# Column blocks of 256 and 225 instead of 251 and 250 in a fused Fourier mixing and MLP kernel

## The chip, the cores and the metric

One core of a Trainium2 chip runs the whole kernel in one launch. The metric is the device time of one execution in microseconds, as the median of several runs. The kernel before takes 1913.87 us.

## The reference

The input `x` is 8 x 3008 x 256, float32. The output is a two-layer MLP with a squared ReLU, applied to the real part of a two-dimensional Fourier transform of each of the eight batches:

```python
X = np.fft.fft(x, axis=1)
X = np.fft.fft(X, axis=2)
h = X.real.reshape(8 * 3008, 256) @ w_in      # w_in: 256 x 2048
g = np.maximum(h, 0.0) ** 2
out = g @ w_out                               # w_out: 2048 x 256
```

## The kernel before

**Two halves.** For each batch b a transform along the sequence makes three tables: `Pt`, `Qt` and `Et`, with 128, 127 and 128 partitions and `NKT` = 1505 columns each, one column for each frequency from 0 to 1504. The transform along the 256 features is multiplied into `w_in` once, at the start (L344, a float32 product with 256 columns of a tile `win`), which gives the weights `G1` and `G2`. The hidden values at frequency k and at its mirror, 3008 - k, are then a sum and a difference of the same two products, so that 1505 columns give 3008 tokens.

**The main loop** runs over the batches (8), over the column blocks of `CK` columns (`BLOCKS`, six a batch: five of 251 and one of 250) and over j (8 pairs of 128 hidden units). One pass through it is a step; there are 384. A step consists of:

- `front`: for each of the two hidden chunks h a product of `Pt` (L881, 128 rows) and one of `Qt` (L882, 127 rows) with `n` columns into one PSUM tile `ph` (two buffers). VectorE then makes the sum and the difference of the two in three instructions (L892, L894, L895), written to a tile `g` with four parts: g11, g12, g21, g22. L895 is the last to read `ph`.
- `relu` and `square` on ScalarE (L906, L909), each over all four parts of `g`.
- `combine` on GpSimd (L916 to L919): four sums of parts of `g` into a tile `s`. They serve a scheme in the manner of Strassen, which makes the second layer with seven products in place of eight.
- `back`, two steps later: seven products (L947) with `n` columns of `g` or `s` into four PSUM tiles `mA` to `mD`, which accumulate over j. (The very first block uses eight plain products, L932.)

So a step has 11 float32 matmuls. The tiles of moving operands are allocated with `CK` columns to a part:

```python
g = gp.tile([P, 2, 2, CK], F32, name="g", tag="g")
s = sp.tile([P, 4, CK], F32, name="s", tag="s")
ks = slice(k0, k0 + n)    # the columns of Pt and Qt in this block
```

With `CK` = 251 part k of `g` or `s` starts at float 251 k of its tile, and block m of `Pt` and `Qt` at float 251 m.

After the eighth j `gather` evicts the four PSUM tiles, and `store` transposes the block on VectorE in squares of 32 (L1018 for the full squares, L1019 for the rest) and sends it out over the SyncE queue, for each of the two mirrored sides. The last block of the kernel is transposed on TensorE instead (L1002).

**The order** is written out by hand. A list of tokens (`ORDER`) sets it for the first ten steps, amid the conversion of the weights. Later, `between` puts pieces of the next batch's fold and transform (L510 to L808) between the steps. Each piece has a written cost, and `pace` and `SHARE` spread them by the number of steps, not by their time; `room` lets in up to 1.9 of these units, meant as microseconds, at once. Neither depends on `CK`.

Of the kernel before, what the change touches and what calls it, by code (L numbers as in the profile page):

```python
# [9 lines left out]
F32 = mybir.dt.float32  # L10
# [4 lines left out]
P = 128  # L15
R = 32
# [46 lines left out]
def column_counts(S):  # L63

    counts = []
    for kp in range(2):
        n0 = len(range(kp, S // 4 + 1, 2))
        n1 = (n0 + 1) // 2
        n2 = (n1 + 1) // 2
        counts.append((n2, n2, n1, n0))  # L70
    return counts
# [12 lines left out]
def kernel(  # L84
# [12 lines left out]
    nc = tc.nc  # L97
# [3 lines left out]
    NKT = M + 1  # L101
# [2 lines left out]
    H = D // 2  # L104
    NJ = NFC // 2
    CH = 256
    CK = 251
    NX = 3
    TILES = class_tiles(S)
    NT = len(TILES)  # L110
    NC = column_counts(S)
# [4 lines left out]
    const = ctx.enter_context(tc.tile_pool(name="const", bufs=1))  # L116
# [3 lines left out]
    pq = ctx.enter_context(tc.tile_pool(name="pq", bufs=2))  # L120
    hp = ctx.enter_context(tc.tile_pool(name="hp", bufs=3))
# [3 lines left out]
    op = ctx.enter_context(tc.tile_pool(name="op", bufs=2))  # L125
# [92 lines left out]
    make_identity(nc, ident)  # L218
    last = ident[:, P - 1:]

    signs = const.tile([P, 2], F32, name="signs")
    for i in range(2):
        nc.vector.tensor_scalar(out=signs[:, i:i + 1], in0=last, scalar1=(-2.0, 2.0)[i], scalar2=(1.0, -1.0)[i],
                                op0=ALU.mult, op1=ALU.add)
# [1 line left out]
    lone = wsum.rearrange("p a j h -> p (a j) h")  # L226
    assert 2 * NT <= 3 * NJ
    nc.gpsimd.memset(lone[:, 0:2 * NT], 0.0)
    evens = const.tile([P, 1], F32, name="evens")
    nc.vector.tensor_reduce(out=evens, in_=ident[:, 0::2], op=ALU.add, axis=mybir.AxisListType.X)  # L230
    for c in range(2):
        nc.vector.tensor_scalar(out=sind[:, c, P - 1:], in0=evens, scalar1=2.0, scalar2=-1.0,
# [28 lines left out]
    def scratch():  # L261

        return sp.tile([P, 4 * CK], F32, name="m", tag="s")[:, 0:2 * CH].rearrange("p (c e) -> p c e", c=2)

# [109 lines left out]
    PQE = {}  # L374
# [35 lines left out]
    def columns(tab, t, part):  # L410

        nk, at = NC[0][TILES[t][0]], PLACE[t]
        nq = (nk + 1) // 2
        return tab[:, 0, at + part * nq:at + (nk if part else nq)]

    def quarters(tab, part):

        nk, at = NC[0][3], PLACE[ODD0]
        n4, n2 = (nk + 3) // 4, (nk + 1) // 2
        return tab[0:HALF2, 0, at + part * n4:at + (n2 if part else n4)]  # L420
# [210 lines left out]
    def dft_ops(b):  # L631
# [1 line left out]


        def start():
            PQE[b] = [pq.tile([n, NKT], F32, name=nm, tag=nm)
                      for nm, n in (("Pt", P), ("Qt", P if b == 0 else P - 1), ("Et", P))]

        def group(kp, which):
            both_in = b == 0 and which == 1  # L640
            n = NE if b is None else P - 1 if which == 1 and b else P
            tab = sinT if which == 1 else cosT
            n2, _, n1, n0 = NC[kp]
            st = {}
# [17 lines left out]

            NK1 = (CK + 1) // 2
            EVEN = ((0, 0, n2), (1, n2, n2), (2, 2 * n2, n1))
# [8 lines left out]
                copy_4()  # L673

            def copy_4():
                a = st["a"] = hp.tile([P, 2 * P], F32, name="da", tag="da", bufs=2)[0:n]
                nc.scalar.copy(a[:, 0:n2], st["ps"][0:n, 0:n2])

            def even_part(c, lone_e, only=None):
# [53 lines left out]
            def left(t):  # L733

                if b is None:
                    return we[0:HALF2, SPOT[t], kp]
                return folded[b, t][0:HALF2, kp, PART[which]][:, 0:n]

            def once_more(ps, nk):

                nq = (nk + 2) // 2 if kp else (nk + 1) // 2
                pair = TWO, TWO + 1
                for part in range(2):
                    if kp:
                        tab, o = (cosT, sinT)[part], 0
                        to = ps[:, part * nq:part * nq + nq]
                    else:
                        tab, o = (cosT, sinT)[which], part
                        to = ps[:, part:nk:2]
                    nc.tensor.matmul(to, left(pair[part != which]),  # L750
                                     columns(tab, TWO, o)[0:HALF2], start=True, stop=True)
                if not kp:
                    return ps[:, 0:nk]
                a = hp.tile([P, NC[0][3] // 2 + 1], F32, name="oc", tag="oc", bufs=1)[0:n, 0:nq]
                nc.scalar.copy(a, ps[:, 0:nq])
                return a, ps[:, nq:2 * nq]

            def twice_more(ps):

                av, aw, bv, bw = (left(ODD0 + i) for i in range(4))
                if kp:
                    nq = (n0 + 2) // 2
                    spots = [(tab, part, ps[:, i * nq + part:(i + 1) * nq:2])
                             for i, tab in enumerate((cosT, sinT)) for part in range(2)]
                    ws = (aw, bw, bv, av) if which else (av, bv, bw, aw)
                else:
                    tab = (cosT, sinT)[which]  # L770
                    spots = [(tab, 0, ps[:, 0:n0:4]), (tab, 1, ps[:, 2:n0:4]),
                             (cosT, 0, ps[:, 1:n0 + 1:4]), (sinT, 0, ps[:, 3:n0:4])]
                    ws = (bw, aw, bv, av) if which else (av, bv, aw, bw)
                for (tab, part, to), w in zip(spots, ws):
                    cols = quarters(tab, part)
                    nc.tensor.matmul(to, w, cols[:, cols.shape[-1] - to.shape[-1]:],  # L776
                                     start=True, stop=True)
                ps_a = ps[:, 0:nq] if kp else ps[:, 5:n0 + 1:4]
                a = hp.tile([P, NC[0][3] // 2 + 1], F32, name="oc", tag="oc", bufs=1)[0:n, 0:ps_a.shape[-1]]
                nc.scalar.copy(a, ps_a)  # L780
                if kp:
                    return a, ps[:, nq:2 * nq]
                st["turned"] = a, ps_a, ps[:, 3:n0:4]
                return ps[:, 0:n0]
# [38 lines left out]
            if b == 0:  # L823
                named = [("copy", copy_4), ("join_4", join_4), ("join_2", join_2), ("lo", lambda: join_lo(0, NK1)),
                         ("keep", keep), ("rest", lambda: join_lo(NK1, n0)), ("hi", join_hi)]
                for e in range(2):
                    for t in range(NT):
                        c = TILES[t][0]
# [13 lines left out]
            return ops  # L842

        ops = [] if b is None else [(0.0, start)]
        for which in (0,) if b is None else (0, 1):
            for kp in range(2):
# [5 lines left out]
    def spread_e():  # L852

        _, qt, et = PQE[0]
        ps = psd.tile([P, CH], F32, name="pe", tag="d")[:, 0:CK]
        nc.tensor.matmul(ps, last.to_broadcast([P, P]), qt[:, 0:CK], start=True, stop=True)
        return lambda: nc.scalar.copy(et[:, 0:CK], ps)

    KH = S // 4 + 1

    def spread_lower():
        _, qt, et = PQE[0]
        nc.gpsimd.dma_start(out=e_dram[0:1, CK:KH], in_=qt[P - 1:P, CK:KH])
        nc.gpsimd.dma_start(out=et[:, CK:KH], in_=e_dram[0:1, CK:KH].to_broadcast([P, KH - CK]))
# [124 lines left out]
    def store(b, k0, n, s, c, final):  # L989

        if s == 0:
            row, lo, hi = b * S + k0, 0, n
        else:
            row, lo, hi = b * S + S - (k0 + n - 1), 1 if k0 + n == NKT else 0, n - 1 if k0 == 0 else n
        if final:


            starts = (lo, n - P)
            po = psd.tile([P, 2, H, 2], F32, name="po", tag="d")
            for h in (1, 0) if s else (0, 1):  # L1000
                for i, o in enumerate(starts):
                    nc.tensor.transpose(po[:, i, :, h], c[:, s, h, o:o + P], ident)  # L1002
            os_ = op.tile([P, 2, H, 2], F32, name="os", tag="os")
            for i in range(2):
                (nc.scalar.copy if s or i else nc.vector.tensor_copy)(os_[:, i], po[:, i])
            left = n - lo - P
            last = n - (left if any(left % k == 0 for k in range(9, 17)) else 15 * (P // 16))
            for i, c0, c1 in ((0, lo, lo + P), (1, last, n), (1, lo + P, last)):
                if c0 < c1:
                    (nc.sync if s or i == 0 else nc.scalar).dma_start(out=out[row + c0:row + c1],  # L1010
                                                            in_=os_[c0 - starts[i]:c1 - starts[i], i])
            return


        full, rest = divmod(hi - lo, R)
        os_ = op.tile([P, full + 1, R, 2], F32, name="os", tag="os")
        to = os_.rearrange("p i e h -> p i h e")
        nc.vector.transpose(to[:, 0:full], c[:, s, :, lo:lo + full * R].rearrange("p h (i r) -> p i h r", r=R))  # L1018
        nc.vector.transpose(to[:, full], c[:, s, :, hi - R:hi])  # L1019
        for a in range(P // R):  # L1020
            rows = out[row + lo:row + hi, 2 * R * a:2 * R * (a + 1)]
            part = os_[R * a:R * (a + 1)].rearrange("r i e h -> r i (e h)")
            nc.sync.dma_start(out=rows[0:full * R].rearrange("(i r) d -> r i d", r=R), in_=part[:, 0:full])
            nc.sync.dma_start(out=rows[full * R:], in_=part[R - rest:, full])

    def ahead(b):
        (_, start), *groups = dft_ops(b)
# [288 lines left out]
    for i in range(NJ + LAG, len(steps) + LAG + 4):  # L1316
        if i < len(steps):
            b, k0, n, j = steps[i]
# [19 lines left out]
        if i < len(steps):  # L1338
            relu(n, g)
            square(n, g)  # L1340
            s, ops = combine(n, g)
# [66 lines left out]
```

## Time and profile before

| | |
|---|---|
| median of three runs | 1913.87 us (1913.75 to 1913.92) |
| profiled execution, first to last instruction (span) | 1911.9 us |
| what lies around the span (median less span) | 2.0 us |
| PE busy | 1902.1 us, 9216 passes |
| VectorE / ScalarE / GpSimd busy | 1444.3 / 959.2 / 1132.0 us |
| first pass of the main loop (L881) | 36.7 us after the start |
| HBM traffic | 41.54 MB read, 24.69 MB written |

Of the profiled execution its span is known; the runs' times take in what lies around it. Busy times are sums of instruction lengths, and the lengths of matmul passes overlap: a pass of 251 columns is listed with 374 ns, and the next one starts some 212 ns after it. For TensorE the distance from start to start is therefore what is counted below. The trace holds the start of every pass to the nanosecond; the timeline prints it to 10 ns.

### The profile page before, as it was taken

To read this page: it belongs to the slowest core of one execution; us is meant where nothing else is said; L and a number is where in the kernel's file an instruction comes from. 1 tells how busy PE (TensorE), PEld (TensorE's weight loads), DVE (VectorE), ACT (ScalarE), POOL (GpSimd) and SP (SyncE) were. 2 spreads that over 40 slices of the span, in tenths; PEclk is the share of its full clock that TensorE was granted. 3 is DMA by queue.
4 is the path that set the end of the run, shared out by engine and by line. 5 is a ranking of instruction groups with operands and counts; after the bars stand their busy time and mean duration, and the time that the engine had idled before them with its cause. 6 is when DMAs were issued, how large, how long until landed. Compare 5 with 4: busy or idle time off the path is not lost.

```text
span 1911.9 us, 28094 instructions
## 1 busy us (share of the span) xinstructions
PE 1902.1 (99%) x9216; PEld 1693.9 (89%) x9216; DVE 1444.3 (76%) x3648; ACT 959.2 (50%) x1220; POOL 1132.0 (59%) x1725
## 2 busy tenths in 40 slices
PE   9999999999999999999999999999999999999998
PEld 7888898888988898888988889888898888988887
DVE  8988887787678776888678877788867777655554
ACT  4755555455455454445445554445544545444444
POOL 3265656665566656665665665566655666566565
PEclk9999999999999999999999999999999999999999
DMA  6341211110112101111011100211101101100100
GB/s 193 119 46 25 52 28 36 30 45 12 35 29 47 28 12 36 34 41 28 12 40 43 37 20 14 52 36 28 25 18 43 36 13 21 28 12 11 22 11 22
DMA packets 144381, 68.08 MB, mean 36 GB/s; under 512 B 129176, under 2 KB 134907, under 8 KB 144234
## 3 DMA queue, kind: packets, MB, share of 16 engines
q1 hardware_dynamic: 143646, 65.47, 14.9%
q8 instruction: 72, 1.18, 0.3%
q0 software_dynamic: 448, 0.69, 0.1%
q14 instruction: 76, 0.61, 0.1%
q10 hardware_dynamic: 139, 0.12, 0.0%
HBM read 41.54 MB, written 24.69 MB: 35 GB/s over the span
## 4 chain that ended last, share of the span: by engine, by line
PE 96%; DVE 2%; DMA 1%; ACT 0%; issue 0%; SPq 0%; DVEq 0%; ACTq 0%
PE ph L881 17%; PE ph L882 17%; PE mC L947 17%; PE mA L947 16%; PE mB L947 16%; PE mD L947 8%; PE pd L776 1%; PE mA L932 1%; PE mB L932 1%; PE pd L750 1%; PE pd L658 1%; PE pg L344 0%; DVE w L540 0%; DVE fs L510 0%; DMA raw<-in_moe_w_out_dram 0%
## 5 line engine op out<-in xcount | busy, mean ns | idle before, releaser
L906 ACT ACTIVATE g<-g 128x1004 f32<-128x1004 f32 (+1 forms) x384 | 399.1, 1039 | 691.6 <-DVE g L895 491.8
L892 DVE SCALAR_TENSOR_TENSOR he<-Et,gE,ph 128x251 f32<-128x251 f32 (+1 forms) x768 | 362.4, 472 | 340.9 <-PE ph L882 337.1
L916 POOL TENSOR_TENSOR s<-g 128x251 f32<-128x251 f32 (+1 forms) x376 | 236.7, 630 | 636.9 <-ACT g L909 587.6
L881 PE MATMUL ph<-Pt,G 128*128 128x251 f32 (+1 forms) x1536 | 452.1, 375 | 0.3 <-DVE g L895 0.3
L882 PE MATMUL ph<-Qt,G 127*128 127x251 f32 (+1 forms) x1536 | 451.2, 374 | 0.0
L909 ACT ACTIVATE g<-g 128x1004 f32<-128x1004 f32 (+1 forms) x384 | 399.1, 1040 | 12.0
L947 PE MATMUL mA<-g,wout 128*128 128x251 f32 (+1 forms) x1488 | 376.8, 374 | 0.0
L947 PE MATMUL mC<-s,wsum 128*128 128x251 f32 (+1 forms) x1472 | 373.2, 374 | 0.0
L894 DVE TENSOR_TENSOR g<-he,ph 128x251 f32<-128x251 f32 (+1 forms) x768 | 320.6, 417 | 53.2 <-POOL s L916 1.4
L882 PEld LDWEIGHTS ph<-Qt,G 127*128 127x128 f32 x1536 | 291.3, 190 | 35.7
L881 PEld LDWEIGHTS ph<-Pt,G 128*128 128x128 f32 x1536 | 285.8, 189 | 34.6 <-ACT G L349 0.7
L895 DVE TENSOR_TENSOR g<-he,ph 128x251 f32<-128x251 f32 (+1 forms) x768 | 314.4, 409 | 0.0
L947 PEld LDWEIGHTS mA<-g,wout 128*128 128x128 f32 x1488 | 279.6, 189 | 34.8 <-issue 0.3
L947 PEld LDWEIGHTS mC<-s,wsum 128*128 128x128 f32 x1472 | 279.5, 190 | 33.6
L917 POOL TENSOR_TENSOR s<-s,g 128x251 f32<-128x251 f32 (+1 forms) x376 | 270.7, 720 | 29.5
L918 POOL TENSOR_TENSOR s<-g 128x251 f32<-128x251 f32 (+1 forms) x376 | 272.6, 725 | 0.0
L919 POOL TENSOR_TENSOR s<-g,s 128x251 f32<-128x251 f32 (+1 forms) x376 | 242.3, 644 | 0.0
L947 PE MATMUL mD<-s,wout 128*128 128x251 f32 (+1 forms) x752 | 220.3, 374 | 0.0
L947 PE MATMUL mB<-s,wout 128*128 128x251 f32 (+1 forms) x752 | 220.0, 374 | 0.0
L947 PE MATMUL mB<-g,wsum 128*128 128x251 f32 (+1 forms) x736 | 215.8, 374 | 0.0
L947 PEld LDWEIGHTS mD<-s,wout 128*128 128x128 f32 x752 | 141.9, 189 | 17.7
L947 PEld LDWEIGHTS mB<-s,wout 128*128 128x128 f32 x752 | 141.6, 188 | 17.3
(204 smaller groups left out, 1424.8 us busy)
## 6 DMA issues: line engine op xcount, KB each, us to landing
out_dram<-os SPq DMA_DIRECT2D x376, 56.0 KB
xt<-in_x_dram SPq DMA_DIRECT2D x39, 384.0 KB
xt<-in_x_dram SPq DMA_DIRECT2D x63, 128.0 KB
Et<-e_dram SPq DMA_DIRECT2D x7, 752.5 KB
out_dram<-os SPq DMA_DIRECT2D x288, 6.8 KB
raw<-in_moe_w_in_dram SPq DMA_DIRECT2D x16, 256.0 KB
raw<-in_moe_w_out_dram SPq DMA_DIRECT2D x16, 256.0 KB
xt<-in_x_dram SPq DMA_DIRECT2D x2, 512.0 KB
```

Of the source, the lines that this page charges most:

```text
L881: nc.tensor.matmul(ps[:, 0, 0:n], G1[:, fs], pt[:, ks], start=True, stop=True)
L882: nc.tensor.matmul(ps[:, 1, 0:n], G2[0:P - 1, fs], qt[0:P - 1, ks], start=True, stop=True)
L892: nc.vector.scalar_tensor_tensor(out=t, in0=PQE[b][2][:, k0:k0 + n], scalar=gE[:, fc:fc + 1], in1=hP, op0=ALU.mult, op1=ALU.add)
L894: tt(out=g[:, h, 0, 0:n], in0=t, in1=hQ, op=ALU.add)
L895: tt(out=g[:, h, 1, 0:n][:, ::-1], in0=t, in1=hQ, op=ALU.subtract)
L906: act(g[:, :, :, 0:n], g[:, :, :, 0:n], AF.Relu)
L909: act(g[:, :, :, 0:n], g[:, :, :, 0:n], AF.Square)
L916: return s, [lambda: gt(out=s1, in0=g21, in1=g22, op=ALU.add), lambda: gt(out=s2, in0=s1, in1=g11, op=ALU.subtract), lambda: gt(out=s3, in ...
L917: lambda: gt(out=s2, in0=s1, in1=g11, op=ALU.subtract),
L918: lambda: gt(out=s3, in0=g11, in1=g21, op=ALU.subtract),
L919: lambda: gt(out=s4, in0=g12, in1=s2, op=ALU.subtract)]
L947: nc.tensor.matmul(acc[nm][:, i, 0:n], w, v[:, 0:n], start=j == 0 and i == 0, stop=j == NJ - 1, skip_group_check=True)
```

## The change

`CK` becomes 256. A batch then has five blocks of 256 columns and one of 225. All parts of `g` and `s` start at multiples of 1024 bytes; the widths of `Pt`, `Qt` and `Et` and of some scratch tiles are rounded up so that every moving operand of the main loop starts at a multiple of 64 bytes. `evens` becomes a column of `signs`. A side of a block that is a multiple of 32 rows needs no second transpose and no second set of output DMAs.

```diff
-    CK = 251
+    CK = 256
...
-    signs = const.tile([P, 2], F32, name="signs")
+    signs = const.tile([P, 3], F32, name="signs")
...
-    evens = const.tile([P, 1], F32, name="evens")
+    evens = signs[:, 2:3]
...
-            PQE[b] = [pq.tile([n, NKT], F32, name=nm, tag=nm)
+            PQE[b] = [pq.tile([n, -(-NKT // 16) * 16], F32, name=nm, tag=nm)[:, 0:NKT]
...
-                a = st["a"] = hp.tile([P, 2 * P], F32, name="da", tag="da", bufs=2)[0:n]
+                a = st["a"] = hp.tile([P, -(-n2 // 16) * 16], F32, name="da", tag="da", bufs=2)[0:n]
...
-                a = hp.tile([P, NC[0][3] // 2 + 1], F32, name="oc", tag="oc", bufs=1)[0:n, 0:nq]
+                a = hp.tile([P, NC[0][3] // 2 + 9], F32, name="oc", tag="oc", bufs=1)[0:n, 0:nq]
...
-            last = n - (left if any(left % k == 0 for k in range(9, 17)) else 15 * (P // 16))
+            last = n - next(m for m in range(left, 0, -1) if any(m % k == 0 for k in range(9, 17)))
...
-        os_ = op.tile([P, full + 1, R, 2], F32, name="os", tag="os")
+        os_ = op.tile([P, full + (rest > 0), R, 2], F32, name="os", tag="os")
...
-        nc.vector.transpose(to[:, full], c[:, s, :, hi - R:hi])
+        if rest:
+            nc.vector.transpose(to[:, full], c[:, s, :, hi - R:hi])
...
-            nc.sync.dma_start(out=rows[full * R:], in_=part[R - rest:, full])
+            if rest:
+                nc.sync.dma_start(out=rows[full * R:], in_=part[R - rest:, full])
```

More of the change, by code (lines that the diff above doesn't have):

```diff
@@ L778, in twice_more @@
                 ps_a = ps[:, 0:nq] if kp else ps[:, 5:n0 + 1:4]
-                a = hp.tile([P, NC[0][3] // 2 + 1], F32, name="oc", tag="oc", bufs=1)[0:n, 0:ps_a.shape[-1]]
+                a = hp.tile([P, NC[0][3] // 2 + 9], F32, name="oc", tag="oc", bufs=1)[0:n, 0:ps_a.shape[-1]]
                 nc.scalar.copy(a, ps_a)
```

## The prediction

> **What bounds the kernel now.** I read the page first, then the list of waits of the matmul engine, then its timeline inside one step, last the starts of single passes in the trace. The page:
>
> ```profile
> span 1911.9 us, 28094 instructions
> ...
> PE 1902.1 (99%) x9216; PEld 1693.9 (89%) x9216; DVE 1444.3 (76%) x3648; ACT 959.2 (50%) x1220; POOL 1132.0 (59%) x1725
> ...
> PEclk9999999999999999999999999999999999999999
> ...
> PE 96%; DVE 2%; DMA 1%; ACT 0%; issue 0%; SPq 0%; DVEq 0%; ACTq 0%
> PE ph L881 17%; PE ph L882 17%; PE mC L947 17%; PE mA L947 16%; PE mB L947 16%; PE mD L947 8%; PE pd L776 1%; PE mA L932 1%; PE mB L932 1%; PE pd L750 1%; PE pd L658 1%; PE pg L344 0%; DVE w L540 0%; DVE fs L510 0%; DMA raw<-in_moe_w_out_dram 0%
> ```
>
> PE is busy for 99% of the span, its granted clock is full in every slice, and the chain that ended last is PE for 96%. A busy PE could still be waiting between matmuls, so the waits of PE come next (engine, line, waited for whom: us, times, longest):
>
> ```profile
> PE pe L856 <- DVE Qt L694: 0.9, 1, 0.9
> ...
> PE ph L881 <- DVE g L895: 0.3, 1, 0.3
> ```
>
> In the main loop PE waited for another engine once, for 0.3 us. So the kernel's time is the sum of the distances from one matmul pass to the next. The timeline of one step (start, length in us; x2 is one float32 matmul, which runs as two passes):
>
> ```profile
> 999.85 0.58 PE L881 MATMUL ph<-Pt,G 128*128 128x251 f32 x2
> ...
> 1001.54 1.01 PE L947 MATMUL mA<-g,wout 128*128 128x251 f32 x4
> 1002.39 0.59 PE L947 MATMUL mB<-g,wsum 128*128 128x251 f32 x2
> 1002.82 0.58 PE L947 MATMUL mB<-s,wout 128*128 128x251 f32 x2
> 1003.24 1.01 PE L947 MATMUL mC<-s,wsum 128*128 128x251 f32 x4
> 1004.09 0.59 PE L947 MATMUL mD<-s,wout 128*128 128x251 f32 x2
> ```
>
> The lengths (0.58 for two passes) overlap; what counts is start to start. Over all undisturbed steps I took the distance from the step's first L881 pass to the next step's: median 4672 ns for 251 columns, 4664 ns for 250. Eleven matmuls make 424.7 ns each.
>
> **What a matmul costs.** Start to start of one matmul (two passes), median ns, in order within the step:
>
> | | Pt | Qt | Pt | Qt | mA g11 | mA g12 | mB g22 | mB s1 | mC s2 | mC s3 | mD s4 |
> |---|---|---|---|---|---|---|---|---|---|---|---|
> | 251 columns | 423 | 426 | 425 | 425 | 425 | 424 | 425 | 422 | 427 | 425 | 425 |
> | 250 columns | 426 | 427 | 426 | 426 | 424 | 420 | 422 | 422 | 428 | 424 | 420 |
>
> The smallest passes are 210.0 ns for 250 columns, 210.8 for 251 and 215.0 for the 256 of L344: 0.833 ns a column (called a tick below) and two ticks, 1.7 ns, fixed (an estimate from these three). Floors per matmul are then 420.0, 421.7 and 430.0. The excess above them goes with where the moving operand starts. In tiles of 251 columns, part k starts at float 251k, that is at 0, 3, 2, 1 floats past a multiple of four. Count the groups of four floats that an operand touches. With 250 columns, operands that touch 63 groups take 420 to 424, those that touch 64 (Pt and Qt of the last block, s2) 426 to 428, near 64 x 4 x 0.833 x 2 = 426.7. With 251 columns, Pt behind mD takes 421.6 to 422.3 in blocks that touch 63 groups and 424.2 to 425.1 where it touches 64; s3 and g12 (64 groups) pass some of it on to the next matmul. A second excess is Qt's: around every L882, which uses 127 rows where its neighbours use 128, the first pass costs some 3.3 ns more, also where the offset was harmless before (Pt at one and the same offset: 421.6 behind mD, 425.2 behind Qt). There are four such changes in a step.
>
> The nearest rows for an aligned 256-column operand are L344's, which read an aligned `win` tile amid the same work:
>
> ```profile
> 54.32 1.02 PE L344 MATMUL pg<-win,sind 128*128 128x256 f32 x4
> 55.19 0.59 PE L881 MATMUL ph<-Pt,G 128*128 128x251 f32 x2
> ```
>
> 0.87 us for two matmuls here; over the 19 undisturbed pairs of this line 430 to 432, mean 431.2, and 433 right behind L882 (218 + 215).
>
> **The sum.** The number of matmuls stays, and so does the sum of columns (5 x 251 + 250 = 5 x 256 + 225 = 1505). PE's order of instructions is the same but for the sizes. So the floor is unchanged, and only the excess can be gained.
> - 256 columns, 64 groups, all aligned: between the floor of 430.0 and the 431.2 of L344 I take the middle, 430.6, since clean 251-column matmuls in the loop lie within 0.6 of their floor. Step: 11 x 430.6 + 4 x 3.3 = 4750 ns. Carrying the old step over column by column gives 4672 + 11 x 2 x 5 x 0.833 = 4764.
> - 225 columns touch 57 groups, 57 x 4 x 0.833 = 190.0 a pass, just over the fitted 189.2. Step: 11 x 380 + 13.3 = 4193 ns. Old step carried over: 4664 - 458 = 4206.
> - Six steps: before 5 x 4672 + 4664 = 28,024; after 5 x 4750 + 4193 = 27,943; 81 ns less, times 8 j times 8 batches = 5.2 us.
> - Bounds: with 430.0 and 378.3 per matmul the steps are 4743 and 4175 and the gain 8.5 us; if the Qt excess went too, 13.6. With 431.7 (a tick more per pass) and 4762, 4212 the gain is 0.1.
>
> A rule that speaks against the change: the Trainium skill, "TensorE: Matmul & The Clock Gate", section "Back-to-back issue gap", makes the distance a function of the column count alone plus a fixed 2.5 ns. By it the sum would be no gain at all, 1913.9 us. The table above, 420 to 428 for the same 250 columns, disagrees. "SBUF — State Buffer" (specifications) states 16-byte lines in SBUF, with a penalty on each crossing to a new one. It gives no price, so the sum doesn't use it.
>
> **Edits that I cost at nothing.** Weight loads: 189 ns each beside passes of 190 looks like a new bound, but it isn't one:
>
> ```profile
> 1629.91 0.86 PE pd L776 x8
> ```
>
> Eight passes with full weights in 0.86 us: 108 ns apart, far below 190. Without that cover the short passes would stay near 212 ns: 22 ns x 22 passes x 64 steps = 31 us. The store: a block of 256 needs one transpose and four DMAs where 251 needed two and eight; the program has 79 fewer DVE transposes (L1019, 0.20 us each, 16 us of DVE) and 316 fewer SP issues. DVE, at 76%, and SP are not on the chain, so nothing is gained there. Padded tiles, `evens` inside `signs`: allocation only. The end: the last block's eviction runs on 225 columns, some five operations of 0.42 us that shrink by 26 ns, 0.1 us. The head of 37 us keeps its order.
>
> The span is 1911.9, the median of the runs 1913.87, 2.0 apart. 1913.87 - 5.2 - 0.1 = 1908.6.
>
> **Rivals.**
> 1. The excess stays (no change): the aligned pass costs 259 ticks (215.8 ns) as half of L344's do, and 225 columns with one float in the last group pay like the 64-group rows. 1913 to 1914. For it: L344 measured 431.2, not 430.0, and 433 behind L882; with those 4764 a step is reached. Against: 421.6 to 422.3 in the loop for aligned operands.
> 2. Slower: the short block starves. Its step is 4.19 us against 4.66, while the work laid beside it (folds and transform of the next batch, spread by step and not by time) stays. DVE needs 2 x (472 + 417 + 409) = 2.60 us a step for the main loop now, some 2.43 at 225 columns, and single side pieces are let in up to 1.9 us: 4.33 is over 4.19. PE would then wait at L881 for a `ph` buffer, and every matmul behind waits with it. In the trace the last read of such a buffer ended mostly 2.0 to 3.2 us before it was needed again in the last block, 0.8 at the worst, which speaks against. The price: 56 such steps (seven batches), so the gain is eaten at 0.09 us a step, and it is measurably slower from 0.16; at 0.2 us it gives 1908.6 + 11.2 = 1919.8.
> 3. A larger gain: 127-row changes cost nothing either once everything is aligned, 1900 to 1904. Against it: Pt at offset 1 or 0 still paid behind Qt.
>
> **How the numbers follow.** The forecast, a gain of 2.4 to 8.5 us, gets 0.62; rival 1, 0.22; rival 2 with other slowdowns, 0.11; rival 3, 0.05. About 0.2% (3.8 us) is what a measurement can tell from no change, so faster means below 1910.0. Of the forecast some 0.52 lies beyond that, with rival 3 that makes 0.57; 0.10 of it and rival 1 make 0.32 the same; 0.11 slower. The likeliest case alone spans 1905.4 to 1911.5; the range for 8 in 10 takes in rival 1 and the foot of rival 2: 1904.0 to 1914.5.
>
> **What would show it.** Steps of 256 columns at 4743 to 4755 ns and short ones at 4175 to 4195 confirm it; every back product at the same 430 to 431; Qt still at +3. Steps at 4762 or more mean rival 1. Waits of PE for DVE at L881, or for POOL at the products, in the short blocks mean rival 2. I am wrong in the reading itself if mC s2 and s3, the dearest now, don't come down to the level of mB s1.

## The result and the profile after

The changed kernel takes 1909.56 us against 1913.75 (medians of 13 runs each): a ratio of 0.9978, 95% interval 0.9970 to 0.9986. That is 4.2 us less; forecast were 5.3, and 1908.6 us in the range 1904.0 to 1914.5. The profiled execution went from 1911.9 to 1907.8 us.

The page of the changed kernel, its busy row, clock and chain:

```profile
span 1907.8 us, 27467 instructions
...
PE 1898.3 (99%) x9216; PEld 1698.5 (89%) x9216; DVE 1469.0 (77%) x3569; ACT 959.7 (50%) x1220; POOL 1210.1 (63%) x1725
...
PEclk9999999999999999999999999999999999999999
...
PE 97%; DVE 1%; DMA 1%; ACT 0%; issue 0%; POOL 0%; DVEq 0%; ACTq 0%
```

PE lost 3.8 us of busy time and is still 97% of the chain that ended last; VectorE and GpSimd are busier than before (1444 and 1132 us), but they make up 1% of that chain or less. In PE's list of waits the main loop's own matmuls have the same single entry as before, in the first batch, and the short blocks have none (us, times, longest):

```profile
PE ph L881 <- DVE g L895: 0.3, 1, 0.3
...
PE pd L776 <- ACT sinT L404: 0.2, 1, 0.2
```

The second line is new: one wait of 0.2 us in a piece of the transform, between two steps of the first batch.

The timeline of a step with 256 columns:

```profile
1093.19 0.59 PE L881 MATMUL ph<-Pt,G 128*128 128x256 f32 x2
...
1094.92 1.03 PE L947 MATMUL mA<-g,wout 128*128 128x256 f32 x4
1095.78 0.59 PE L947 MATMUL mB<-g,wsum 128*128 128x256 f32 x2
1096.21 0.59 PE L947 MATMUL mB<-s,wout 128*128 128x256 f32 x2
1096.65 1.03 PE L947 MATMUL mC<-s,wsum 128*128 128x256 f32 x4
1097.51 0.59 PE L947 MATMUL mD<-s,wout 128*128 128x256 f32 x2
1097.94 0.38 PE L881 MATMUL ph<-Pt,G 128*128 128x256 f32 x1
```

From Pt to Pt 4.75 us. And the products with 225 columns, at the seam to the next batch:

```profile
982.27 0.54 PE L947 MATMUL mB<-g,wsum 128*128 128x225 f32 x2
982.65 0.54 PE L947 MATMUL mB<-s,wout 128*128 128x225 f32 x2
983.03 0.92 PE L947 MATMUL mC<-s,wsum 128*128 128x225 f32 x4
983.79 0.54 PE L947 MATMUL mD<-s,wout 128*128 128x225 f32 x2
```

0.38 us apart. From the starts of the single passes, the median distance per matmul in ns, in the columns of the prediction's table:

| | Pt | Qt | Pt | Qt | mA g11 | mA g12 | mB g22 | mB s1 | mC s2 | mC s3 | mD s4 | step |
|---|---|---|---|---|---|---|---|---|---|---|---|---|
| 256 columns | 432 | 435 | 434 | 433 | 433 | 430 | 432 | 432 | 432 | 432 | 432 | 4755 |
| 225 columns | 380 | 383 | 382 | 382 | 382 | 378 | 380 | 380 | 380 | 380 | 380 | 4187 |

The spread over the products (420 to 428 ns before) is gone; what differs is the first Qt and the four matmuls behind it. Six steps take 5 x 4755 + 4187 = 27,962 ns. For the kernel before the prediction put them at 28,024; counted over all 276 undisturbed steps with 251 columns the median is 4674 ns, not 4672, and six steps take 28,034. The difference is 72 ns, times 64 it is 4.6 us. The trace as a whole, with the steps that side work disturbs, gives a little less: from the first step of the second batch to that of the eighth a batch takes 230.83 us in place of 231.39. That is 0.55 us a batch, 4.4 us for eight. The main loop begins 0.2 us later than before (36.9 against 36.7 us), and 4.2 us remain. So the gain came out of the main loop, where PE's passes follow each other faster; that this is due to alignment is for the experiments to show.

### The profile page after: what moved, and what is told of

Read it like the earlier page. It is cut to its first block, busy times and chain, and to the rows that moved or that the text cites. A ratio compares the mean times of both kernels' runs of the same rounds, so it can differ in the third digit from the quotient of the medians.

```text
span 1907.8 us, 27467 instructions
## 1 busy us (share of the span) xinstructions
PE 1898.3 (99%) x9216; PEld 1698.5 (89%) x9216; DVE 1469.0 (77%) x3569; ACT 959.7 (50%) x1220; POOL 1210.1 (63%) x1725
## 4 chain that ended last, share of the span: by engine, by line
PE 97%; DVE 1%; DMA 1%; ACT 0%; issue 0%; POOL 0%; DVEq 0%; ACTq 0%
PE ph L881 17%; PE ph L882 17%; PE mA L947 16%; PE mB L947 16%; PE mC L947 16%; PE mD L947 8%; PE pd L658 2%; PE pd L776 1%; PE mA L932 1%; PE mB L932 1%; PE pd L750 1%; PE pg L344 1%; DMA xt<-in_x_dram 0%; DMA cosT<-in_cos_s_dram 0%; DVE he L892 0%; DVE g L895 0%
## 5 line engine op out<-in xcount | busy, mean ns | idle before, releaser
L906 ACT ACTIVATE g<-g 128x1024 f32<-128x1024 f32 (+1 forms) x384 | 399.5, 1040 | 689.1 <-DVE g L895 340.9
L916 POOL TENSOR_TENSOR s<-g 128x256 f32<-128x256 f32 (+1 forms) x376 | 271.0, 721 | 562.1 <-ACT g L909 465.0
L892 DVE SCALAR_TENSOR_TENSOR he<-Et,gE,ph 128x256 f32<-128x256 f32 (+1 forms) x768 | 360.9, 470 | 313.9 <-PE ph L882 310.7
L881 PE MATMUL ph<-Pt,G 128*128 128x256 f32 (+1 forms) x1536 | 452.4, 376 | 0.3 <-DVE g L895 0.3
L882 PE MATMUL ph<-Qt,G 127*128 127x256 f32 (+1 forms) x1536 | 451.3, 374 | 0.0
L909 ACT ACTIVATE g<-g 128x1024 f32<-128x1024 f32 (+1 forms) x384 | 399.5, 1041 | 12.0
L947 PE MATMUL mA<-g,wout 128*128 128x256 f32 (+1 forms) x1488 | 376.8, 374 | 0.0
L947 PE MATMUL mC<-s,wsum 128*128 128x256 f32 (+1 forms) x1472 | 371.9, 375 | 0.0
L894 DVE TENSOR_TENSOR g<-he,ph 128x256 f32<-128x256 f32 (+1 forms) x768 | 319.3, 416 | 53.0 <-POOL s L916 0.5
L895 DVE TENSOR_TENSOR g<-he,ph 128x256 f32<-128x256 f32 (+1 forms) x768 | 313.0, 408 | 0.0
L917 POOL TENSOR_TENSOR s<-s,g 128x256 f32<-128x256 f32 (+1 forms) x376 | 270.9, 720 | 29.5
L919 POOL TENSOR_TENSOR s<-g,s 128x256 f32<-128x256 f32 (+1 forms) x376 | 276.5, 735 | 0.0
L918 POOL TENSOR_TENSOR s<-g 128x256 f32<-128x256 f32 (+1 forms) x376 | 273.7, 728 | 0.0
```

The source lines that it names most:

```text
L881: nc.tensor.matmul(ps[:, 0, 0:n], G1[:, fs], pt[:, ks], start=True, stop=True)
L882: nc.tensor.matmul(ps[:, 1, 0:n], G2[0:P - 1, fs], qt[0:P - 1, ks], start=True, stop=True)
L892: nc.vector.scalar_tensor_tensor(out=t, in0=PQE[b][2][:, k0:k0 + n], scalar=gE[:, fc:fc + 1], in1=hP, op0=ALU.mult, op1=ALU.add)
L894: tt(out=g[:, h, 0, 0:n], in0=t, in1=hQ, op=ALU.add)
L895: tt(out=g[:, h, 1, 0:n][:, ::-1], in0=t, in1=hQ, op=ALU.subtract)
L906: act(g[:, :, :, 0:n], g[:, :, :, 0:n], AF.Relu)
```

## The experiments

The theory: the gain is the price of moving operands that start off a group of four floats (16 bytes). The rivals: the counts 256 and 225 are good by themselves; 64 bytes is the unit; Qt's excess has another cause than its 127 rows. Two versions of the theory fell on the way. The ratios are to the kernel before, run anew beside each set of experiments (medians 1913.52 us for runs 1 to 4, 1913.44 for 5 to 8, 1913.47 for 9 and 10). All runs but the fifth are variants of the changed kernel and so carry its other edits, the padded tables and `evens` inside `signs`.

**1. Only the parts of `g` and `s` aligned, blocks of 251.**

```diff
-    CK = 256
+    CK = 251
+    CW = 256
-        return gp.tile([P, 2, 2, CK], F32, name="g", tag="g")
+        return gp.tile([P, 2, 2, CW], F32, name="g", tag="g")
-        s = sp.tile([P, 4, CK], F32, name="s", tag="s")
+        s = sp.tile([P, 4, CW], F32, name="s", tag="s")
```

> Blocks of 251 and 250 columns as before, but the parts of g and s lie 256 floats apart, so that every product of back reads an operand that starts a group of four floats; Pt and Qt stay at multiples of 251. Theory (a pass that touches one group of four floats more costs up to 4 ticks more): g12, g22, s2, s3, s4 fall to some 421.7 ns each, mA g11 stays at 425 behind Qt, the step falls from 4672 to about 4654, and the time is about 1907.4 us: below the changed kernel, though no column count changed. Rival (the gain comes from the counts 256 and 225 themselves, the start is without effect): the products stay at 424 to 427, the time at 1913.8.

Measured: 1910.98 us, ratio to before 0.9987 (0.9978 to 0.9996). The products did become equal, but at 423 ns, not 421.7; the step is 4665. Without any change of a column count 2.5 us of the gain are there (in the trace 0.39 us of the 0.55 a batch), so the counts 256 and 225 are not what brings them. The timeline from the first product to the next step's Pt, first of the kernel before, then of this run:

```profile
1001.54 1.01 PE L947 MATMUL mA<-g,wout 128*128 128x251 f32 x4
...
1004.52 0.58 PE L881 MATMUL ph<-Pt,G 128*128 128x251 f32 x2
```

```profile
1000.22 1.01 PE L948 MATMUL mA<-g,wout 128*128 128x251 f32 x4
...
1003.18 0.59 PE L882 MATMUL ph<-Pt,G 128*128 128x251 f32 x2
```

2.98 against 2.96 us; by the means over all such steps 2974 against 2964 ns for the seven products. The size was missed: the floor of 253 ticks that I had read off mB s1 isn't held by a row of aligned products. They take 254, three ticks more than their columns.

**2. The same with parts 252 floats apart** (`CW = 252`), so that all start a group of 16 bytes, but three of four no multiple of 64.

> As the run with parts 256 floats apart, but 252 apart: every part starts a group of 16 bytes, and three of four do not start a multiple of 64 bytes. If 16 bytes is the unit: the same products at 421.7 ns and the same 1907.4 us. If 64 bytes is: those at 252, 504 and 756 floats keep an excess of 2 to 5 ns, and the time lies between 1910 and 1913.

Measured: 1910.85 us, 0.9986 (0.9977 to 0.9995), the products at 423 ns and the step at 4665, as in run 1 to the nanosecond. For the products 16 bytes is enough.

**3. All matmuls of a step with 127 rows.**

```diff
-        nc.tensor.matmul(ps[:, 0, 0:n], G1[:, fs], pt[:, ks], start=True, stop=True)
+        nc.tensor.matmul(ps[:, 0, 0:n], G1[0:P - 1, fs], pt[0:P - 1, ks], start=True, stop=True)
...
-            nc.tensor.matmul(acc[nm][:, i, 0:n], w, v[:, 0:n], start=j == 0 and i == 0, stop=j == NJ - 1,
+            nc.tensor.matmul(acc[nm][:, i, 0:n], w[0:P - 1], v[0:P - 1, 0:n], start=j == 0 and i == 0, stop=j == NJ - 1,
```

> The changed kernel with 127 rows in every matmul of front and back (row 127 of the contraction is left out, so the output is not the reference's): no change of row count within a step. Theory (the change between 127 and 128 rows costs some 3.3 ns in the first pass behind it): Qt, the Pt behind it and mA g11 fall from 433 to 435 to the 432 or 430 of their neighbours, 7 to 15 ns a step, 2.7 to 5 us in all, 1904.5 to 1907. Rival (the excess belongs to the ph tile or to what front waits for, and not to the rows): the same first passes of 218 to 220 ns, 1909.6.

Measured: 1906.89 us, 0.9966 (0.9953 to 0.9978). Every matmul of a 256-column step takes 432 ns (216 + 216) and the step 4748; with 225 columns 380 and 4180. Qt's excess is the change of row count. Removing it saves 7 ns a step, the lower end: in the changed kernel the first pass behind a change takes 218 to 220 ns in place of 216, but the passes after it take 215 until the row has settled.

**4. Qt with 128 rows from the second batch on**, with a zero row.

```diff
-                      for nm, n in (("Pt", P), ("Qt", P if b == 0 else P - 1), ("Et", P))]
+                      for nm, n in (("Pt", P), ("Qt", P), ("Et", P))]
+            if b:
+                nc.gpsimd.memset(PQE[b][1][P - R:P], 0.0)
...
+        rows = P if b else P - 1
-        nc.tensor.matmul(ps[:, 1, 0:n], G2[0:P - 1, fs], qt[0:P - 1, ks], start=True, stop=True)
+        nc.tensor.matmul(ps[:, 1, 0:n], G2[0:rows, fs], qt[0:rows, ks], start=True, stop=True)
```

> The changed kernel with 128 rows in L882 from the second batch on: row 127 of Qt is set to zero there by a GpSimd memset for each batch, the product is the same. Theory: as with 127 rows everywhere, 7 to 15 ns a step in 336 of 384 steps, 1905 to 1907.3 us. Rival: no change, 1909.6, or slower by the memset if it holds up the queue of GpSimd.

Measured: 1907.79 us, 0.9970 (0.9959 to 0.9982), half a microsecond above the expected range and the fastest full computation of this study. Its page and the memset (count | busy us, mean ns | idle before):

```profile
span 1905.9 us, 27481 instructions
...
L639 POOL MEMSET Qt<- 32x1505 f32 x7 | 9.4, 1350 | 0.4
```

The seven memsets are hidden; from the second batch on the steps are at 4748 and 4180 ns, as in run 3.

**5. The kernel before with blocks of 253.**

```diff
-    CK = 251
+    CK = 253
```

> The kernel before with one line changed: CK = 253 in place of 251 (five blocks of 253 and one of 240, nothing aligned). New form of the theory, after the first four runs: a pass takes the larger of n + 3 ticks and 4 ticks for each group of four floats that its operand touches. With 253 columns no start can touch more than 64 groups, 256 ticks, which is n + 3: every matmul should take 426.7 ns wherever it starts, the step 11 x 426.7 + 7 = 4700 ns, six steps 27,965 ns as in the changed kernel (27,962), and the time 1909.6 us without any alignment. Rival (a start off 16 or 64 bytes costs for itself, as 251 columns suggested): matmuls of 429 to 430 ns, 1913.5 us.

Measured: 1912.39 us, 0.9995 (0.9986 to 1.0004); not told apart from before, and a miss. Pt and Qt did as expected (425, 430, 429, 429, little off aligned operands), but the products take 428, 425, 430, 425, 430, 429, 429 and the step 4709. A touched group too many can't be the reason at 253 columns, where each start touches 64 groups. A reason that is left is that the starts differ from one product to the next; run 9 tests it. Not every change of start costs: g12 (two floats past a group, behind g11 at none) and s1 (at none, behind g22 at three) took 425.

**6. The changed kernel with blocks of 252 and 245** (`CK = 252`).

> The changed kernel with CK = 252 (five blocks of 252 and one of 245): every moving operand starts a group of 16 bytes, most do not start a multiple of 64 bytes, and no block has 256 columns. Theory: n + 3 ticks a pass, 425.0 and 413.3 ns a matmul, steps of 4682 and 4554, 27,964 in six, 1909.6 us. If 64 bytes matters for Pt and Qt, or the count 256 does: 1911 to 1913.5.

Measured: 1909.45 us, 0.9979 (0.9970 to 0.9988): products of 425 and 413 ns, steps of 4682 and 4555, six of them 27,965 ns. That is the changed kernel's gain (4.0 us here against 4.2), without the count 256 and without 64 bytes.

**7. The changed kernel with parts 257 floats apart** (`CW = 257` as in run 1, `CK` left at 256).

> The changed kernel with the parts of g and s 257 floats apart: g12, g22 and most of s start off a group of four, Pt and Qt stay aligned. Theory: 65 groups are 260 ticks against n + 3 = 259, so 256-column products off a group take 433.3 ns in place of 431.7, 4 to 5 of the seven, some 8 ns a step; 225 columns touch 57 groups from any start and stay at 380. In all 2 to 3 us, 1911.6 to 1912.6. Rival (any misaligned start costs 2 to 5 ns a matmul, as with 251): also in the short blocks, 5 us, 1914 to 1915. If alignment has no part in it: 1909.6.

Measured: 1910.82 us, 0.9986 (0.9977 to 0.9995), 1.3 us above the changed kernel; 2 to 3 were expected. The loop itself did as expected: a batch takes 0.26 us more than in the changed kernel, 2.1 us for eight, but the main loop began 0.5 us earlier and the first batch was quicker. The products of 256 columns take 433, 430, 435, 430, 433, 433, 434, those of 225 take 382, 378, 382, 379, 381, 379, 382. Dear first passes (218 to 220 ns) alternate with passes of 215, a tick less than aligned ones take. That passes gain a tick back behind a dear one had not been in the expectation, and neither had the 3 ns that the products of the short blocks lose, which touch 57 groups from any start.

**8. One look at the price by columns**, all products aligned.

```diff
-    BLOCKS = [(k0, min(CK, NKT - k0)) for k0 in range(0, NKT, CK)]
+    BLOCKS = [(0, 256), (256, 255), (511, 254), (765, 253), (1018, 252), (1270, 235)]
```

> One look at the price by columns: the changed kernel with blocks of 256, 255, 254, 253, 252 and 235 columns, the products of back all aligned. Theory: their pairs of passes take 2 (n + 3) ticks: 431.7, 430.0, 428.3, 426.7, 425.0, 396.7 ns. If whole groups of four are paid for: 431.7 for the first four, 425.0, 398.3. Pt and Qt start at 0, 3, 1, 2 floats past a group from the second block on and follow max(n + 3, 4 x groups): only 255 and 254 columns with a start of 0 and 3 matter, 254 at 3 touches 65 groups, 260 ticks, 433.3 ns.

Measured, in one run of 1910.49 us: the products settle at 432, 430, 428, 427, 425 and 397 ns: two passes of n + 3 ticks each, with no rounding to groups. Pt with 254 columns from three floats past a group takes 433 as expected, 260 ticks for 65 groups. Two blocks that the expectation had passed over follow the same count: Pt with 252 columns from two floats past a group takes 427 (64 groups, 256 ticks), with 235 columns 399 (60 groups make 400).

**9. Blocks of 253, every part one float past a group.**

```diff
-    CK = 256
+    CK = 253
+    CW, AT = 256, 1
-        return gp.tile([P, 2, 2, CK], F32, name="g", tag="g")
+        return gp.tile([P, 4 * CW + 4], F32, name="g", tag="g")[:, AT:AT + 4 * CW].rearrange(
+            "p (a c k) -> p a c k", a=2, c=2)
-        s = sp.tile([P, 4, CK], F32, name="s", tag="s")
+        s = sp.tile([P, 4 * CW + 4], F32, name="s", tag="s")[:, AT:AT + 4 * CW].rearrange("p (i k) -> p i k", i=4)
```

> CK = 253 again, with the parts of g and s 256 floats apart and all of them one float past a group of four: every product of back is misaligned, and in the same way. With 253 columns one float past touches 64 groups, 256 ticks, n + 3. Theory (max(n + 3, 4 x groups) within a run of operands that start alike, and something more only where the start changes from one operand to the next, which the run with 253 columns at mixed starts showed as 429 to 430): products at 426.7 ns, step 4700, 1909.6 us. Rival (a misaligned operand costs for itself whatever stands before it): products at 429 to 430, step 4709 or more, 1912.4 or more.

Measured: 1909.82 us, 0.9981 (0.9972 to 0.9990), the step at 4701 and the products behind the row change at 427. All products are misaligned here, and nothing is lost. The timeline from the first product to the next step's Pt, first of run 5 (mixed starts), then of this run:

```profile
1000.46 1.02 PE L947 MATMUL mA<-g,wout 128*128 128x253 f32 x4
...
1003.46 0.59 PE L881 MATMUL ph<-Pt,G 128*128 128x253 f32 x2
```

```profile
999.98 1.02 PE L949 MATMUL mA<-g,wout 128*128 128x253 f32 x4
...
1002.97 0.59 PE L882 MATMUL ph<-Pt,G 128*128 128x253 f32 x2
```

3.00 against 2.99 us; by the means over all such steps 2996 against 2987 ns for the seven products. (Run 5 also lacks the change's other edits; Pt and Qt, whose blocks start at the same columns in both runs, take about the same in sum, 1713 and 1714 ns a step.)

**10. Blocks of 251, every part three floats past a group** (`CK = 251`, `AT = 3`).

> CK = 251 with the parts of g and s 256 floats apart and all three floats past a group: 64 groups from any of them, 256 ticks against n + 3 = 254. Theory: all products at 426.7 ns (250 columns: 253 and 3 floats, 64 groups, 426.7 as well), the step 4687 to 4690 in place of 4665 with the same parts aligned, some 5 to 8 us more than that run: 1916.5 to 1919. Rival (only a change of start costs): 1911, as aligned.

Measured: 1914.59 us, 1.0005 (0.9996 to 1.0014): 3.6 us more than the same blocks aligned (run 1), less than expected. Products of 250 columns take 425 ns (255 ticks a pass) where aligned ones take 422, those of 251 take 424 to 425 where aligned ones take 423. So a touched group too many costs also where all starts are alike: two ticks a pass with 250 columns, and some half a tick with 251, where 4 x 64 = 256 would have been three and two.

## Why the prediction was right

**The bound.** PE's distances from pass to pass made the time before and after; no wait in the main loop took the place of the gain. That step held.

**The source.** The excess of misaligned operands goes when they are aligned: run 1 moved the starts of `g` and `s` at the old column counts and gave 2.5 us. Run 6, with Pt and Qt on 16 bytes too, gave 1.4 us more than run 2, which has the products alone aligned; before, Pt and Qt took 426 to 427 ns with 250 columns, where they touch 64 groups. Run 7 moved the parts off again and lost part of the gain. mC s2 and s3 came down to the level of mB s1, as the prediction's last section had asked.

**The terms that were mis-sized.** The forecast of 5.3 us came near the 4.2 measured in part by luck, since errors of opposite sign met in the sum.
- 256 columns: 430.6 per matmul was taken, between a floor of two ticks and L344's 431.2. Settled aligned products take 431.7 (259 ticks, three above the columns; run 8 shows the three at every size). The clean 421.7 of the old loop, on which the middle rested, was no floor of a settled row: such passes stood behind dear ones. Eleven matmuls at 1.1 ns more are 12 ns a step, which alone would have taken 3.8 us off the gain.
- The row changes: 4 x 3.3 = 13.3 ns were charged; run 3 shows 7, because the passes behind a dear one win part of it back. That gives 2.4 us back. With both, 11 x 431.7 + 7 = 4756, and 4755 was measured.
- 225 columns: 380.0 per matmul was right, and for the wrong reason. I had 57 groups x 4 ticks = 228; it is 225 + 3 = 228. With 7 in place of 13.3 the step is 4187, as measured.
- The step before: 4672 ns holds for the first block of a batch; over all blocks it is 4674. That is 10 ns in six steps, 0.6 us of gain that the sum didn't have. The later start of the main loop, 0.2 us, was not in it either.

The Trainium skill's rule that was weighed against the change ("TensorE: Matmul & The Clock Gate", section "Back-to-back issue gap") is given there for a matmul by itself: the number of columns divided by 2.4, plus 2.5 ns. A float32 pass here takes twice that per column, 0.833 ns. With that rate in the rule it fits the settled aligned passes exactly: 215.8 ns for 256 columns and 190.0 for 225. What the rule leaves out is the start of the operand, on which the gain rests, and the change of rows, which cost 7 ns a step in the changed kernel.

**The rivals.** Rival 1 was right that the aligned pass costs 259 ticks and wrong that the step reaches 4764: it takes 4755. Rival 2 did not happen: PE's list has no wait in the short blocks, and the last read of a `ph` buffer there ended at least 0.75 us before the buffer's next use (0.80 before). Rival 3 did not happen either: with everything aligned the row changes still cost 7 ns a step. Run 3 shows what they are worth, 2.7 us, where the 13.3 ns charged would have made 5.

**Costed at nothing.** The weight loads stayed hidden beside passes of 190 ns. The saved transposes bring nothing, as expected: run 6 kept them all (3648 VectorE instructions, as before) and gained as much. VectorE's busy time rose nevertheless, by 25 us.

**What stays open** is the exact rule for misaligned starts. Touched groups explain runs 8 and 9 and the blocks of Pt and Qt; a change of start between neighbours explains run 5 against run 9, though two of run 5's changes cost nothing; but run 10 is cheaper than 4 ticks a group, and in run 7 part of each dear pass is gained back and the short blocks lose 3 ns that no group explains. A rule that gives all of these to the tick was not found.

## What to carry to other kernels

When the chain is one engine at 99% without waits, look at the distances from start to start of its instructions and sort them by operand: a few ns that repeat thousands of times are the whole headroom. For float32 matmuls here, let moving operands start on 16 bytes, and keep the row count equal from matmul to matmul, if need be with a zero row. Starts that are misaligned but all alike cost nothing with 253 columns (run 9) and 3.6 us with 251 and 250 (run 10), so they are no substitute. Once all starts were on 16 bytes, blocks of 252 and 245 did as well as 256 and 225, with the same number of blocks. And don't take the smallest spacing in a disturbed stream for the floor: it may be the recovery behind a dear one.

## What the runs showed that I had not expected

A dear first pass is partly paid back: behind it passes run at n + 2 ticks, in the changed kernel for the three behind mA's first (218, then 215, 215, 215 ns), before the row settles at n + 3 (216).

GpSimd slowed down where PE gained. The sum L916 of two parts of `g`, before and after (columns as in the list of groups):

```profile
L916 POOL TENSOR_TENSOR s<-g 128x251 f32<-128x251 f32 x312 | 196.8, 631 | 518.5 <-ACT g L909 472.9 <-DVE he L892 23.3 <-PE ph L882 13.6
```

```profile
L916 POOL TENSOR_TENSOR s<-g 128x256 f32<-128x256 f32 x312 | 228.6, 733 | 470.9 <-ACT g L909 377.7 <-PE ph L882 46.7 <-DVE os L1018 27.5
```

631 to 733 ns for 2% more columns. In run 1, with 251 columns and aligned parts, the same sum takes 722, in run 7, with 256 columns 257 apart, 637, and in run 9, all one float off, 726. So it goes with how the parts lie and not with the count; which pairs are dear, and why, was not worked out. VectorE's busy time goes the same way: 1444 us before, 1473 in run 1, 1437 in run 7. In all GpSimd's busy time rose by 78 us with the change (1132 to 1210). Here that is hidden; where GpSimd bounds a kernel it would not be.
